# A transformer block on one core: attention jobs of 4 heads x 256 queries, softmax denominators inverted on a reshaped tile by way of DRAM, b2 on GpSimd, last chunk split in two

## The chip, the cores and the metric

The kernel runs on one core of a Trainium2 chip. Times are device microseconds (us) of one execution. "Before" has a median of 1203.07 us over three runs (1201.48 to 1203.55). Engines: PE is TensorE (PEld its weight loads), DVE is VectorE, ACT is ScalarE, POOL is GpSimd, SP is SyncE, which here issues every DMA.

## The reference

One pre-norm transformer block in bf16 with S = 2048 tokens, D = 1024, 32 heads of 32, F = 3584:

```python
h  = x + softmax(q @ k.T * 32**-0.5) @ v @ wo        # q, k, v from layernorm(x) @ wqkv, per head
h2 = h + gelu_tanh(layernorm(h) @ w1 + b1) @ w2 + b2
```

## The kernel before

The kernel is a list of tasks with dependencies. A small scheduler inside the kernel plays them through with assumed durations, and from that fixes the order in which each engine executes its tasks. On the chip every engine then works off its own list in that order, waiting on semaphores.

Attention runs in chunks of 512 queries. Under the attention of one chunk, PE also does "background" work: the projections (chunk 0), then Wo, layer norm, FFN1 and FFN2 of the chunk before. The background has one PSUM bank (7). The last chunk's Wo and FFN run alone after attention: the tail. One attention job is 2 heads x 512 queries. A PV unit is four concurrent matmuls of 512 columns: two for O, two (with a stationary tile of ones) for the softmax denominators.

```python
    def proj(which, g, tc, bank, evac, direct=False):
        ...                                     # psum -> stg (bf16), then for K:
            for pr in range(2):
                for half in range(2):           # four 64x256 copies into KT2
                    dve(lambda v, pr=pr, half=half: v.tensor_copy(
                        KT2[64 * half:64 * half + 64, 2 * g + pr, tc, :, :],
                        stg[64 * pr:64 * pr + 64, s, 256 * half:256 * half + 256]), ...)
        ...
        def pv_unit(self, bank, first, last):
            ...
            for j in range(2):
                fns.append(lambda p, j=j, h=h: p.matmul(psum[32 * j:32 * j + 32, bank, :],
                    V[:, kt, 32 * h:32 * h + 32], PT[:, s, j, :], ...))
            for j in range(2):
                fns.append(lambda p, j=j: p.matmul(psum[64 + 32 * j:96 + 32 * j, bank, :],
                    ones32[:, :], PT[:, s, j, :], ...))
            ...
        def finish(self, qc, g, pr, bank):
            dve(... Dsb[64 * pr:64 * pr + 64, :] <- psum[64:128, bank, :] ...)     # shortened
            dve(... Osb[64 * pr:64 * pr + 64, :] <- psum[0:64, bank, :] ...)       # shortened
            if (qc, g, 1 - pr) in self.fin:
                for k in range(4):
                    dve(lambda v, k=k: v.reciprocal(Dsb[:, 128 * k:128 * k + 128], Dsb[:, 128 * k:128 * k + 128]), 0.93, ...)
                ...
                    dve(lambda v: v.tensor_tensor(OT[:, qc % 2, g, :], Osb[:, :], Dsb[:, :], ALU.mult), ...)
    ...
    def ffn2(R, qc, banks):
        ...                                     # b2 enters as one more matmul of each group
                mm(bank, two_row[:, :], b2t[:, 512 * j:512 * j + 512], True, False, ...)
```

The softmax here doesn't subtract the row's maximum and nothing guards it: scores larger than these inputs give would overflow.

## Time and profile before

The profile of before: per-core view (span, granted clock):

```profile
core 0: 1417.9 us, clock 0.749
```

and the first part of its page (busy us, share of the span, instructions):

```profile
PE 1366.2 (96%) x17326; PEld 510.9 (36%) x17336; DVE 673.2 (47%) x1165; ACT 1085.3 (77%) x1189; POOL 37.9 (3%) x96
```

In that profile PE is the limit, but the span is 215 us longer than the timed runs, so it does not show what limits those. The timeline (start, duration, instruction, count, idle time before) shows Exps back to back at 16.60 / 18 = 0.922 us.

```profile
1238.44 16.60 ACT L643 ACTIVATE PT<-ps 128x1024 bf16<-128x1024 f32 x18 [0.22 <-PE ps L634]
```

The chain of waits (start, duration, what) shows 13 groups of four concurrent 256-column matmuls in 1.92 us (0.148 each), and 49 full 512-column matmuls in 14.08 us (0.287 each):

```profile
93.05 1.92 PE ps L439 x52
...
1328.24 14.08 PE ps L443 x49
```

```profile
PE 1126.7 (94%) x17326; PEld 465.2 (39%) x17336; DVE 668.4 (56%) x1165; ACT 1059.2 (88%) x1189; POOL 38.2 (3%) x96
```

The last PV matmul of this profile ends at 1074.0 us. The windows view splits the span there: attention, then the tail (each entry is the engine's busy time in the window):

```profile
core 0: us, PE busy (x) PEld busy (x) DVE busy (x) ACT busy (x) POOL busy (x), PEclk, DMA share, GB/s
25.00:1074.00 1049.00, 991.55 (x16506) 396.06 (x16495) 578.60 (x989) 1013.24 (x1120) 23.41 (x56) 1.00 0.31 92
1074.00:1201.00 127.00, 114.46 (x533) 52.89 (x539) 71.08 (x130) 37.89 (x60) 6.45 (x16) 0.96 0.28 87
```

Under attention ACT is busy 1013 of 1049 us and PE 992: both are nearly full, and neither has room for much more. In the tail PE alone carries the time.

### The profile page before, as it was taken

How to read it: one execution, taken by the hardware profiler on the slowest of the kernel's cores; microseconds unless marked ns; L12 is line 12 of the kernel's file. 1: busy time of each engine (PE TensorE's matmuls, PEld its weight loads, DVE VectorE, ACT ScalarE, POOL GpSimd, SP SyncE). 2: the span in 40 equal slices, each digit the busy share in tenths (PEclk: the TensorE clock that was granted, in tenths of full speed). 3: DMA queues.
4: the chain of work that ended last, by engine and by line, in shares of the span. 5: the costliest groups of instructions: out<-in, count | busy, mean ns of one | idle time of the engine just before them, and what ended most of it. 6: DMA issues, size and time to landing. Idle time of an engine off the chain costs nothing.

```text
span 1417.9 us, 37847 instructions
## 1 busy us (share of the span) xinstructions
PE 1366.2 (96%) x17326; PEld 510.9 (36%) x17336; DVE 673.2 (47%) x1165; ACT 1085.3 (77%) x1189; POOL 37.9 (3%) x96
## 2 busy tenths in 40 slices
PE   8999999999999999999999999999999999978999
PEld 5544443433333333332333333333333333324333
DVE  7354444443546774223547762225677612245710
ACT  4778787878888888888888888888988888844500
POOL 2000000000100000000100000000000000001000
PEclk7777777777777777777777777777777777766777
DMA  6800000025343222303342230422323322202222
GB/s 165 224 2 13 28 13 14 13 72 156 101 122 101 76 69 72 124 16 98 107 124 71 83 98 16 124 71 63 107 73 98 102 66 85 87 0 75 74 93 71
DMA packets 165793, 112.29 MB, mean 79 GB/s; under 512 B 25345, under 2 KB 162817, under 8 KB 164866
## 3 DMA queue, kind: packets, MB, share of 16 engines
q1 hardware_dynamic: 165634, 109.87, 26.2%
q8 instruction: 136, 2.23, 0.7%
q14 instruction: 23, 0.19, 0.1%
HBM read 98.58 MB, written 11.27 MB: 77 GB/s over the span
## 4 chain that ended last, share of the span: by engine, by line
PE 91%; ACT 4%; DVE 3%; issue 1%; POOL 1%; DMA 0%; POOLq 0%; DVEq 0%
PE ps L439 48%; PE ps L654 17%; PE ps L634 12%; PE ps L443 10%; ACT PT L643 3%; PE ps L658 2%; PE ps L798 1%; ACT xnT L512 1%; DVE a_xh L748 1%; PE ps L508 1%; DVE V L606 0%; DVE stg L547 0%; DVE Osb L668 0%; DVE Dsb L666 0%; DMA a_w1r<-in_A_wqkv_dram 0%
## 5 line engine op out<-in xcount | busy, mean ns | idle before, releaser
L643 ACT ACTIVATE PT<-ps 128x1024 bf16<-128x1024 f32 x1024 | 989.2, 1025 | 180.5 <-PE ps L634 166.1
L654 PE MATMUL ps<-PT,V 128*32 128x512 bf16 x2048 | 383.4, 457 | 13.7 <-DVE V L606 6.2
L658 PE MATMUL ps<-PT,ones 128*32 128x512 bf16 x2048 | 384.8, 458 | 0.0
L439 PE MATMUL ps<-a_w2r,gT 128*32 128x512 bf16 x2688 | 241.9, 452 | 0.0
L634 PE MATMUL ps<-QT,KT 32*128 32x512 bf16 x2048 | 216.7, 414 | 7.4 <-ACT PT L643 7.3
L439 PE MATMUL ps<-a_hnT,a_w1r 128*32 128x512 bf16 x2688 | 215.2, 454 | 4.0 <-DVE a_xh L748 3.2
L654 PEld LDWEIGHTS ps<-PT,V 128*32 128x32 bf16 x2048 | 103.3, 104 | 143.9 <-issue 89.3
L634 PEld LDWEIGHTS ps<-QT,KT 32*128 32x128 bf16 x2048 | 51.5, 91 | 272.3 <-ACT PT L643 164.5
L439 PE MATMUL ps<-xnT,Wall 128*32 128x512 bf16 x1344 | 111.6, 453 | 7.0 <-ACT xnT L512 4.8
L439 PEld LDWEIGHTS ps<-a_w2r,gT 128*32 128x32 bf16 x2688 | 77.3, 109 | 112.0 <-issue 103.3
L673 DVE RECIPROCAL Dsb<-Dsb 128x128 f32<-128x128 f32 x128 | 115.1, 928 | 1.0
L439 PEld LDWEIGHTS ps<-a_hnT,a_w1r 128*32 128x32 bf16 x2688 | 70.6, 107 | 108.0 <-issue 71.4
L782 DVE SCALAR_TENSOR_TENSOR a_ost<-ps,hch 128x512 bf16<-128x512 f32 x24 | 16.6, 692 | 189.8 <-PE ps L439 189.7
L658 PEld LDWEIGHTS ps<-PT,ones 128*32 128x32 bf16 x2048 | 103.5, 104 | 6.6 <-issue 6.6
L748 DVE TENSOR_SCALAR a_xh<-ps,b1f 128x512 bf16<-128x512 f32 x84 | 63.1, 751 | 81.3 <-PE ps L439 80.2
L666 DVE COPY Dsb<-ps 64x512 f32<-64x512 f32 x64 | 44.4, 694 | 101.5 <-PE ps L658 100.1
L439 PE MATMUL ps<-Wall,xnT 128*32 128x256 bf16 x2048 | 83.8, 314 | 0.0
L547 DVE CAST stg<-ps 128x512 bf16<-128x512 f32 x40 | 27.5, 689 | 89.2 <-PE ps L439 89.2
L443 PE MATMUL ps<-a_hnT,b_w1r 128*128 128x512 bf16 x219 | 64.5, 470 | 2.1 <-ACT a_hnT L512 1.5
L439 PEld LDWEIGHTS ps<-Wall,xnT 128*32 128x32 bf16 x2048 | 57.6, 107 | 22.7 <-issue 11.3
L443 PE MATMUL ps<-a_w2r,gT 128*128 128x512 bf16 x219 | 64.1, 461 | 0.5
L439 PE MATMUL ps<-a_w1r,OT 128*32 128x512 bf16 x768 | 63.1, 453 | 0.8 <-DVE hch L719 0.5
(69 smaller groups left out, 875.5 us busy)
## 6 DMA issues: line engine op xcount, KB each, us to landing
a_w2r<-in_B_w_dram SPq DMA_DIRECT2D x56, 512.0 KB, 4.6
a_w1r<-in_B_w_dram SPq DMA_DIRECT2D x42, 512.0 KB, 3.9
a_w1r<-in_A_wo_dram SPq DMA_DIRECT2D x16, 512.0 KB, 4.7
QT<-q_scratch SPq DMA_DIRECT2D x60, 128.0 KB, 2.8
b_w1r<-in_B_w_dram SPq DMA_DIRECT2D x14, 512.0 KB, 3.8
a_w1r<-in_A_wqkv_dram SPq DMA_DIRECT2D x11, 512.0 KB, 5.1
xrb<-in_A_x_dram SPq DMA_DIRECT2D x16, 256.0 KB, 3.9
Wall<-in_A_wqkv_dram SPq DMA_DIRECT2D x16, 256.0 KB, 5.4
```

What stands on the lines that cost most here:

```text
L439: fns.append(lambda p, j=j: p.matmul(psum[32 * j:32 * j + 32, bank, c0:c1], lhsT[:, 32 * j:32 * j + 32], rhs, start=start, stop=stop, tile ...
L443: pe(lambda p: p.matmul(psum[:, bank, c0:c1], lhsT, rhs, start=start, stop=stop), occ, reads=reads, writes=[B_ps[bank]], mode="full")
L508: pe(lambda p, dc=dc: p.transpose(psb[:, bank, dc * P:(dc + 1) * P], src_ap[:, dc * P:(dc + 1) * P], ident[:]), 0.064, reads=[B_src, B_ide ...
L547: dve(lambda v: v.tensor_copy(stg[:, s, :], psum[:, bank, :]), c_dve_ps(512), reads=[B_ps[bank]], writes=[B_stg[s]])
L634: return p.matmul(psum[:, 2 * u + j, :], KT2[r0:r0 + 32, p16, tc, i, :], QT2[r0:r0 + 32, qs, pr, :], start=True, stop=True, tile_position= ...
L643: act(lambda a, u=u, s=s: a.activation(PT[:, s, :, :], psum[:, 2 * u:2 * u + 2, :], ACT.Exp, bias=0.0, scale=SCALE), 1024, reads=[B_ps[2 * ...
L654: fns.append(lambda p, j=j, h=h: p.matmul(psum[32 * j:32 * j + 32, bank, :], V[:, kt, 32 * h:32 * h + 32], PT[:, s, j, :], start=first, st ...
L658: fns.append(lambda p, j=j: p.matmul(psum[64 + 32 * j:96 + 32 * j, bank, :], ones32[:, :], PT[:, s, j, :], start=first, stop=last, tile_po ...
L666: dve(lambda v: v.tensor_copy(Dsb[64 * pr:64 * pr + 64, :], psum[64:128, bank, :]), c_dve_ps(512), reads=[B_ps[bank]], writes=B_Dsb[pr], p ...
L673: dve(lambda v, k=k: v.reciprocal(Dsb[:, 128 * k:128 * k + 128], Dsb[:, 128 * k:128 * k + 128]), 0.93, reads=[B_Dsb[0][k], B_Dsb[1][k]], w ...
L748: dve(lambda v, i=i, fc=fc, bank=bank: v.tensor_scalar(R.xh[:, i, :], psum[:, bank, :], b1f[:, fc:fc + 1], None, ALU.add), c_dve_ps(512), ...
L782: dve(lambda v, o=o, t4=t4, j=j, bank=bank: v.scalar_tensor_tensor(R.ost[:, o, :], psum[:, bank, :], 0.5, hch[:, t4, 512 * j:512 * j + 512 ...
```

## The change

The intent, item by item:

- **Shape.** A job is 4 heads x 256 queries. K and Q are used as projected (no K/Q copies on DVE). O fills columns 0 to 255 of a bank and the denominators columns 256 to 511, on the same partitions, so one DVE copy evacuates both. Matmuls have 256 columns, and there are twice as many.
- **Reciprocals.** A DVE reciprocal of 128x128 takes 0.928 us in before, one of 128x8 takes 0.200 us in after. The 4 x 256 distinct denominators of a job are therefore written to DRAM, read back as 128 x 8, inverted, written again, and read back broadcast.
- **b2** is added by GpSimd instead of by a matmul.
- **Split.** The last chunk of 512 becomes two of 256, to halve the tail.

```diff
+    CH = [(0, 512), (512, 512), (1024, 512), (1536, 256), (1792, 256)]
     ... (proj, load_q, qk, wo, ln2, ffn1 follow the new shapes; cut)
         def pv_tile(self):
+            for den in range(2):
+                for h in range(4):
+                    fns.append(lambda p, h=h, den=den: p.matmul(
+                        psum[32 * h:32 * h + 32, job.bank, 256 * den:256 * den + 256],
+                        ones32[:, :] if den else V[:, kt, P * job.g + 32 * h:P * job.g + 32 * h + 32],
+                        PT[:, ss[h // 2], h % 2, 256 * i:256 * i + 256], ...))
         def finish(self, job):
+            dve(lambda v: v.tensor_copy(OD[:, o, :], psum[:, job.bank, :]), ...)
+            if qc == LAST and g == G - 1:
+                ...                     # the very last jobs still invert on DVE: 2 x 128x128
+                return
+            dma(dd[n].rearrange("(h t) -> h t", h=4), OD[0:P:32, o, 256:512], 4096, ...)
+            dma(Rc[:, o, :], dd[n].rearrange("(p e) -> p e", p=P), 4096, ...)
+            dve(lambda v: v.reciprocal(Rc[:, o, :], Rc[:, o, :]), 0.15, ...)
+            dma(rd_[n].rearrange("(p e) -> p e", p=P), Rc[:, o, :], 4096, ...)
+            for h in range(4):
+                dma(Rb[32 * h:32 * h + 32, b, :], rd_[n:n + 1, 256 * h:256 * h + 256].broadcast_to((32, 256)), 32768, ...)
+            dve(lambda v: v.tensor_tensor(OT[:, qc % 2, g, c0:c0 + 256], OD[:, o, 0:256], Rb[:, b, :], ALU.mult), ...)
     def ffn2(R, qc, banks):
-                mm(bank, two_row[:, :], b2t[:, 512 * j:512 * j + 512], True, False, ...)
+                dve(... R.th[:, f, :] <- psum * 0.5 + hch ...)          # shortened
+                pool(lambda g, ...: g.tensor_tensor(R.ost[:, o, :], R.th[:, f, :], b2t[:, 512 * j:512 * j + 512], ALU.add), 1.1, ...)
```

## The prediction

> **What bounds it now.** The profiled span is 1417.9 us, the timed median 1203.07. The per-core view gives a granted TensorE clock of 0.749; in the profile PE is the limit: 96% busy, 91% of the chain of waits, ACT 77%. A 512-column matmul takes 0.287 us back to back (49 in 14.08 us). The Trainium skill ("TensorE: Matmul & The Clock Gate", Part 1) gives 2.4 GHz as the full clock and says one or two busy cores never trip its 13/16 limiter; this one-core trace is at 0.75 all the same. I infer that the timed runs have a clock near 1. Estimate then: back-to-back Exp of 128x1024 take 0.922 us (18 in 16.60, timeline), x1024 = 944 us; tanh and evacuations before the tail add about 65; first Exp at 27 us: attention ends no earlier than 1030. The tail (1257 to 1418 in the trace, mostly matmuls) would be 128. That is 1160 of 1203; the other 45 are rounds where PE comes late (QK, two PV groups and about five background groups fill a round as well as two Exps do). So ACT and PE jointly until attention ends, then PE and DVE.
>
> **What the change does.**
> - Exps and matmul columns of attention: unchanged. Twice the matmuls, of 256 columns. Those already ran at 0.148 us per group of four (52 in 1.92 us) against 0.142 ideal: about 12 us more over the PV groups; QK with twice the weight loads 0 to 25 us. Partly behind ACT.
> - DVE: minus 115 us reciprocals, 28 K copies, 44 (one OD copy for Dsb and Osb), plus some 15: 673 to about 500. But waits released by DVE cost PE only 27 us of idle time. Worth 0 to 12 us.
> - b2: 32 matmul groups less, 7 to 9 us, a quarter in the tail; the add goes to idle POOL.
> - Reciprocal via DRAM: four dependent transfers of about 2 us (128 KB landed in 1.7 to 2.8 here), 9 us per job of 16. Off the path, except that SyncE is blocked meanwhile.
> - Last chunk split: hoped for, half a tail (60 us). But PE has little room under attention: in the new instruction order, after the last attention matmul there remain 64 group equivalents of narrow FFN1, 112 of narrow FFN2, 32 of Wo and 224 of the last FFN: 432 against 521. Narrow FFN1 has one bank and 2.7 us of DVE per two blocks, so 22 us; then 31 + 3; last FFN1 (14 x 2.25 us, DVE-bound) 32; FFN2 24; end 5: 118 against 128. The layer-norm gap (1270 to 1284) is filled by the FFN2 before it. About 10 us, not 60.
> - Head: first Exp 1 to 2 us earlier.
>
> **Sum.** 1203 - 10 (tail) - 2 - 5 (b2 in attention) - 6 (DVE) + 10 (smaller matmuls) = 1190 us, 8 in 10 between 1160 and 1222. Faster by over 2%: 0.30; within 2%: 0.62; slower: 0.08. In a profile at clock 0.75, about 1410.
>
> **What shows it.** DVE near 500 us; reciprocal group under 20; Exp group near 990; PV within 5% of before; QK under 0.1 us longer per round; after the last Exp still over 130 us at clock 0.75, with narrow FFN matmuls in it; POOL adds near 1 us; OT product about 10 us behind the OD copy.
>
> **What would make it wrong.** Timed clock not near 1; 256-column matmuls bound by weight loads or issue at full clock (slower by 30 us or more); Q loads stuck behind the reciprocal chain on SyncE; or the shorter DVE queue and single evacuation removing most of the 45 us of late rounds (faster, to 1160).

## More of the kernel before

After the prediction I took another profile of the unchanged kernel; it fell at clock 0.993 and is the one to compare with:

```profile
core 0: 1200.7 us, clock 0.993
```

## The result, and the profile after

After has a median of 1223.35 us (1219.28 to 1223.96, four runs); before, beside it, 1202.89. The ratio is 1.016 (95% interval 1.0143 to 1.0178). A ratio here is the mean time of one kernel's fast runs over that of the other's of the same rounds, so it is not quite the ratio of the medians. After is 20 us slower, just above the range I gave, and clear of the noise. All outputs are right.

The profile of after, same three views as for before:

```profile
core 0: 1217.5 us, clock 0.988
```

```profile
PE 1130.9 (93%) x24704; PEld 593.1 (49%) x24704; DVE 524.8 (43%) x976; ACT 1048.7 (86%) x1173; POOL 74.9 (6%) x126
```

```profile
25.00:1094.00 1069.00, 1007.85 (x23056) 515.86 (x23052) 438.39 (x804) 1017.21 (x1124) 54.63 (x88) 0.99 0.34 100
1094.00:1218.00 124.00, 102.19 (x1360) 61.40 (x1348) 66.00 (x126) 22.62 (x39) 12.33 (x16) 0.95 0.61 187
```

The last PV matmul ends at 1094.4 us, 20.4 us later than before; the tail is 123.1 us instead of 126.7. The loss lies under attention. There ACT has 4 us more work and PE 16 us more, but the window is 20 us longer, and DVE, which had been the target of the saving, is busy 140 us less. An engine with less to do cannot be the cost by its own busy time, so one looks for who waits.

The fourth part of the page (shares of the chain that ended last, by engine), before at clock 0.993:

```profile
PE 74%; ACT 11%; DVE 11%; DMA 2%; issue 1%; POOL 1%; SPq 0%; POOLq 0%; DVEq 0%
```

and after:

```profile
PE 61%; DMA 17%; DVE 10%; ACT 6%; SPq 4%; issue 2%; POOL 0%; POOLq 0%; DVEq 0%; ACTq 0%
```

DMA and SyncE's queue went from 2% to 21% of the chain. DVE's waits in after (who waited for what: us in total, times, longest):

```profile
DVE OT L697 <- DMA Rb<-r_scratch: 149.4, 53, 9.2
DVE Rc L692 <- DMA Rc<-d_scratch: 96.7, 43, 8.6
```

DVE stands still for 246 us on the chain through DRAM. DVE's idle time as such costs nothing. What matters is whether something urgent stands behind the waiting instruction. The timeline of after shows that it can:

```profile
501.96 0.39 PE L445 MATMUL ps<-a_w2r,gT 128*32 128x512 bf16 x4
...
502.50 0.40 PE L639 MATMUL ps<-QT,KT 32*128 32x256 bf16 x8
503.55 0.42 DVE L697 TENSOR_TENSOR OT<-OD,Rb 128x256 bf16<-128x256 f32 x1 [9.22 <-DMA Rb<-r_scratch]
503.90 0.68 DVE L806 SCALAR_TENSOR_TENSOR a_th<-ps,hch 128x512 f32<-128x512 f32 x1
504.50 0.68 DVE L679 COPY OD<-ps 128x512 f32<-128x512 f32 x1
504.63 0.83 PE L445 MATMUL ps<-a_w2r,gT 128*32 128x512 bf16 x12 [1.74 <-DVE a_th L806]
```

The background group in bank 7 (L445) is finished at 502.35. Its evacuation (L806) could start then, but on DVE it stands behind the OT product (L697), which has waited 9.22 us for its transfer and starts at 503.55. So the bank comes free over 1 us late, and PE's next background matmul starts at 504.63 after 1.74 us of idle time. The Trainium skill ("TensorE: Matmul & The Clock Gate", section "Architectural detail: the array is 16x 32x32, not 1x 128x128") says that ACT and DVE queues are strict FIFO; this trace agrees, since nothing passed the waiting product. A count over the trace finds about 20 such places under attention, with over 0.3 us between the end of the last background matmul and its evacuation behind an OT product or Rc reciprocal that had waited for its transfer; they add up to about 18 us.

The second pattern is at the start of a chunk, where Wo of the chunk before begins with the last head group (g = 7). The chain of waits in after at 550 us:

```profile
550.12 0.69 DVE a_th L806
550.82 0.61 DVE OD L679
551.42 0.02 issue
551.44 1.85 DMA d_scratch<-OD
553.29 0.02 issue
553.30 2.09 DMA Rc<-d_scratch
555.40 0.02 issue
555.42 0.21 DVE Rc L692
555.63 0.02 issue
555.65 1.63 DMA r_scratch<-Rc
...
558.60 2.69 DMA Rb<-r_scratch
...
561.41 0.43 DVE OT L697
561.84 0.04 issue
561.89 1.46 PE ps L445 x9
```

From the start of the OD copy to the OT product it takes 10.6 us: four dependent transfers of 1.6 to 2.7 us, and 1.3 us in which SyncE issues the first three of the four broadcasts before the last can start. This was one of the shorter chains: the 53 OT products that waited for their transfer started 9.0 to 18.7 us after the end of their OD copy, 12.0 in the median. Until 561.89 PE has no background matmul; it does only QK and PV, has idle gaps, and runs at half clock for 6.8 us from 557.7 us of the span (the records of the granted clock; 10.2 us more from 817.1, at the next chunk start). No single idle gap of PE from 30 us to the end of attention is longer than 2.0 us; in the 3.4 us before each of these two stretches PE was busy for 1.8 us. ACT stays busy until near the end of the first stretch; between 563 and 565 us it does nothing. PE is busy for 1008 of the 1069 us of attention already, so postponed background work comes back later, as Exps that wait for QK or as a longer tail.

### The profile page after: what moved, and what is told of

It reads as the page before. It is cut to its first block, busy times and chain, and to the rows that moved or that the text cites. A ratio compares the mean times of both kernels' runs of the same rounds, so it can differ in the third digit from the quotient of the medians.

```text
span 1217.5 us, 52938 instructions
## 1 busy us (share of the span) xinstructions
PE 1130.9 (93%) x24704; PEld 593.1 (49%) x24704; DVE 524.8 (43%) x976; ACT 1048.7 (86%) x1173; POOL 74.9 (6%) x126
## 4 chain that ended last, share of the span: by engine, by line
PE 61%; DMA 17%; DVE 10%; ACT 6%; SPq 4%; issue 2%; POOL 0%; POOLq 0%; DVEq 0%; ACTq 0%
PE ps L445 37%; PE ps L664 11%; PE ps L639 9%; DMA Rb<-r_scratch 5%; ACT PT L651 4%; DMA r_scratch<-Rc 4%; SPq L466 4%; DMA Rc<-d_scratch 3%; PE ps L449 3%; DVE a_xh L769 3%; DMA d_scratch<-OD 2%; DVE a_uu L778 1%; ACT xnT L516 1%; DMA a_w2r<-in_B_w_dram 1%; PE ps L824 1%
## 5 line engine op out<-in xcount | busy, mean ns | idle before, releaser
L664 PE MATMUL ps<-PT,V 128*32 128x256 bf16 x4096 | 257.3, 275 | 16.1 <-ACT PT L651 11.5
L664 PE MATMUL ps<-PT,ones 128*32 128x256 bf16 x4096 | 256.0, 274 | 0.0
L445 PE MATMUL ps<-a_hnT,a_w1r 128*32 128x512 bf16 (+1 forms) x3584 | 202.3, 354 | 25.8 <-DVE a_xh L769 24.1
L445 PE MATMUL ps<-a_w2r,gT 128*32 128x512 bf16 x3136 | 218.9, 381 | 3.5 <-DVE a_th L806 2.8
L639 PE MATMUL ps<-QT,KT 32*128 32x256 bf16 x4096 | 204.7, 274 | 7.2 <-ACT PT L651 6.5
L445 PEld LDWEIGHTS ps<-a_hnT,a_w1r 128*32 128x32 bf16 x3584 | 84.3, 96 | 105.4 <-DVE a_xh L769 33.0
L445 PEld LDWEIGHTS ps<-a_w2r,gT 128*32 128x32 bf16 x3136 | 71.8, 96 | 66.4 <-issue 29.8
L769 DVE TENSOR_SCALAR a_xh<-ps,b1f 128x512 bf16<-128x512 f32 (+1 forms) x112 | 76.4, 682 | 52.2 <-PE ps L445 51.1
L445 PE MATMUL ps<-xnT,Wall 128*32 128x512 bf16 x1344 | 89.2, 381 | 7.7 <-ACT xnT L516 5.1
L697 DVE TENSOR_TENSOR OT<-OD,Rb 128x256 bf16<-128x256 f32 x63 | 26.8, 425 | 149.5 <-DMA Rb<-r_scratch 149.4
L780 ACT ACTIVATE a_th<-a_uu 128x512 f32<-128x512 bf16 x98 | 62.1, 634 | 33.8 <-DVE a_uu L778 33.5
L809 POOL TENSOR_TENSOR a_ost<-a_th,b2t 128x512 bf16<-128x512 f32 x28 | 32.5, 1161 | 667.1 <-DVE a_th L806 656.9
L445 PE MATMUL ps<-Wall,xnT 128*32 128x256 bf16 x2048 | 70.2, 274 | 2.7 <-DVE V L603 2.3
L782 DVE SCALAR_TENSOR_TENSOR gT<-a_th,a_xh 128x512 bf16<-128x512 f32 x98 | 66.7, 681 | 7.2 <-ACT a_th L780 6.7
L778 DVE SCALAR_TENSOR_TENSOR a_uu<-a_sq,a_xh 128x512 bf16<-128x512 bf16 x98 | 67.6, 690 | 2.6
L445 PE MATMUL ps<-a_w1r,OT 128*32 128x512 bf16 x896 | 62.9, 397 | 5.9 <-DVE OT L697 4.4
L679 DVE COPY OD<-ps 128x512 f32<-128x512 f32 x64 | 43.9, 687 | 39.2 <-PE ps L664 38.3
L445 PEld LDWEIGHTS ps<-Wall,xnT 128*32 128x32 bf16 x2048 | 50.0, 96 | 16.9 <-issue 9.0
```

The lines of the kernel that those rows point to most:

```text
L445: fns.append(lambda p, j=j: p.matmul(psum[32 * j:32 * j + 32, bank, c0:c1], lhsT[:, 32 * j:32 * j + 32], rhs, start=start, stop=stop, tile ...
L639: return p.matmul(psum[:, 2 * us[h // 2] + h % 2, 256 * i:256 * i + 256], KT[32 * h:32 * h + 32, NCH * job.g + tc, P * k4:P * k4 + P], QT[ ...
L664: fns.append(lambda p, h=h, den=den: p.matmul(psum[32 * h:32 * h + 32, job.bank, 256 * den:256 * den + 256], ones32[:, :] if den else V[:, ...
L679: dve(lambda v: v.tensor_copy(OD[:, o, :], psum[:, job.bank, :]), c_dve_ps(512), reads=[B_ps[job.bank]], writes=[B_OD[o]], prio=-1)
L769: dve(lambda v, i=i, fc=fc, bank=bank, c=c: v.tensor_scalar(R.xh[:, i, c], psum[:, bank, c], b1f[:, fc:fc + 1], None, ALU.add), c_dve_ps(w ...
L778: dve(lambda v, i=i: v.scalar_tensor_tensor(R.uu[:, i, :], R.sq[:, i, :], C2, R.xh[:, i, :], ALU.add, ALU.mult), c_dve(512), reads=[R.B_sq ...
```

## The experiments

Time of the n-th Exp's start (us), read from the traces; every kernel has 1024 Exps of the same size, 256 of them per 512 queries. The last columns are the end of the last PV matmul and the tail after it.

| profile of | Exp 1 | 257 | 513 | 769 | 1024 | last PV ends | tail |
|---|---|---|---|---|---|---|---|
| before (clock 0.993) | 23.9 | 299.9 | 557.6 | 815.1 | 1070.6 | 1074.0 | 126.7 |
| after | 22.4 | 297.5 | 560.8 | 829.1 | 1092.7 | 1094.4 | 123.1 |
| e1 reciprocals on DVE | 22.2 | 295.0 | 555.8 | 813.0 | 1072.1 | 1074.4 | 119.6 |
| e4 longer latencies | 21.8 | 294.1 | 552.0 | 810.7 | 1073.6 | 1076.0 | 128.0 |
| e5 product and reciprocal on GpSimd | 22.3 | 295.4 | 558.4 | 820.5 | 1086.2 | 1088.3 | 124.9 |
| e6 e1 without split | 22.1 | 294.6 | 552.5 | 809.3 | 1064.9 | 1066.8 | 125.1 |
| e7 shape alone | 22.0 | 294.4 | 552.5 | 808.8 | 1064.5 | 1066.5 | 125.3 |
| e8 = e4 + g = 7 on DVE | 21.7 | 296.1 | 554.0 | 814.6 | 1077.0 | 1079.2 | 113.5 |
| e10 g = 7 on DVE | 21.9 | 296.5 | 559.5 | 825.0 | 1089.8 | 1091.8 | 112.4 |
| e11 = e5 + e10 | 22.5 | 299.4 | 560.8 | 820.5 | 1085.5 | 1087.5 | 110.4 |

After is not behind until Exp 257, that is while chunk 0 runs with projections in the background; it loses from the first chunk start on.

My theory at this point: the reciprocal's way through DRAM is the loss. Rivals: the split with its extra weight traffic (132 MB moved on the DMA queue against 110), or the 256-column matmuls. One thing holds for every experiment: the scheduler builds the order of all engines anew, so each edit also reshuffles instructions that it does not name. e2 and e3 below, which leave the chain alone, moved the time by 0 and 2.5 us; gains of 10 us and more are well above that, differences of a few us are not.

**b0_before: before unchanged, for a profile at the same clock.**

> The kernel before, unchanged, for a profile at the same granted clock as the one of after (0.99). All theories: about 1202 us, clock over 0.97. My estimate was that its tail (from the last PV matmul to the end) is 128 us, so attention ends near 1075 us; after has 123 and 1094. If attention here ends near 1075, the loss of the change (about 20 us) lies wholly under attention, and the tail gained about 5 us. If it ends near 1095, the loss lies in the tail. [...]

Measured: 1202.52 us (one run, so of unknown state), clock 0.993, attention to 1074.0, tail 126.7. The loss lies under attention. (This run has two half-clock stretches as well, but elsewhere: from about 1067 us, where attention ends, and from about 1090 us, in the tail.)

**e1_recip: reciprocals on DVE.**

```diff
-            dma(dd[n]...); dma(Rc[:, o, :]...); dve(reciprocal Rc); dma(rd_[n]...); 4 x dma(Rb[...])
+            for k in range(2):
+                dve(lambda v, k=k: v.reciprocal(Rb[:, b, P * k:P * k + P], OD[:, o, 256 + P * k:256 + P * k + P]), 0.93, ...)
```

> After, with the reciprocals on DVE again (two of 128x128 per job, 0.93 us each) in place of the four dependent transfers through DRAM. Theory 1 (the reciprocal's way through DRAM delays OT at chunk starts and blocks SyncE's queue): 1190 to 1205 us, 20 to 30 us faster than after, the clock dips at chunk starts gone. Rival 2 (the split last chunk and its weight traffic cost the time): within 8 us of 1223. Rival 3 (256-column matmuls are what costs): within 8 us of 1223, or slower because DVE gets 105 us more work.

Measured: 1193.99 us, ratio to before 0.9931 (0.9914 to 0.9948). Against after that is 0.0229 of 1203, or 27.5 us, with 93 us more work on DVE:

```profile
PE 1125.1 (94%) x24701; PEld 594.9 (50%) x24704; DVE 617.6 (52%) x1039; ACT 1046.3 (88%) x1173; POOL 74.5 (6%) x126
```

The theory's number came in. Not quite as forecast: two dips of the clock remain, from 304.6 and 799.5 us of the span, 3.4 us each. The dips are not the cause of the loss: 17.0 us at half clock under attention (after) cost PE at most 8.5 us of full-clock time, and e11 below has 20.4 us of them and no loss.

**e2_nosplit: four chunks of 512 again.**

```diff
-    CH = [(0, 512), (512, 512), (1024, 512), (1536, 256), (1792, 256)]
+    CH = [(0, 512), (512, 512), (1024, 512), (1536, 512)]
```

> After, with four chunks of 512 again (only the split of the last chunk undone). Rival 2 (the split costs: 20 MB more weights, DMA waits of 5 to 7 us in the tail, single-bank FFN1 after the last attention): 1200 to 1210 us. Theory 1 (DRAM reciprocal): 1222 to 1235 us, because the split as such saved about 5 to 10 us. Rival 3 (256-column shape): the same 1222 to 1235.

Measured: 1220.97 us, ratio 1.0161, the same as after's 1.0160. The rival that blames the split falls (1220.97 is also 1 us under the band of the theory). So does my own estimate that the split saves 5 to 10 us; e6 takes that up.

**e3_b2mm: b2 as a matmul again.**

```diff
+                mm(bank, two_row[:, :], b2t[:, 512 * j:512 * j + 512], True, False, ...)
-                pool(... R.ost <- R.th + b2t ...)
```

> After, with b2 as a matmul again (32 more groups of 512 columns, no GpSimd add). All theories: 1223 to 1232 us, 0 to 9 us slower than after (40 groups of 0.22 us are 8.8 us if all on the path). If it is faster, the GpSimd add (1.16 us, behind a DVE instruction in the ring of th) was itself a cost.

Measured: 1219.91 us, ratio 1.0139 (1.0119 to 1.0158). The interval overlaps that of after, and 1219.91 is just under the forecast band, so b2's move is worth nothing that these runs resolve, and certainly not the 7 to 9 us I had estimated. (The 40 groups in the expectation are a slip for 32.)

**e4_lat: the same instructions, in an order built on longer latencies.** Only the scheduler's assumption is changed, by 1.5 us for each of the chain's transfers:

```diff
-            t.done = max(state["dma"], s0) + dma_lat - 0.9
+            t.done = max(state["dma"], s0) + dma_lat - 0.9 + t.extra      # extra = 1.5 for the chain's DMAs
```

> After with no instruction changed: only the scheduler is told that each of the chain's transfers takes 1.5 us longer than it assumed, so that the small reciprocal and the OT product stand later in DVE's fixed order, and the dependent transfers later in SyncE's. e1 (reciprocals on DVE) showed that the way through DRAM costs 29 us. Theory 1a (the loss is head-of-line blocking: DVE idles 246 us behind late transfers, with evacuations of the background bank behind it, because the order was built on too short a latency): 1198 to 1212 us, DVE's wait for Rb and Rc falls below 100 us. Theory 1b (the loss is the latency of the chain itself, OT late at chunk starts and at the end): 1218 to 1235 us, as now or worse.

Measured: 1204.35 us, ratio 1.0008 (0.9993 to 1.0023): 18.3 us faster than after with the same instructions in another order. DVE's waits on the chain halved:

```profile
DVE OT L700 <- DMA Rb<-r_scratch: 70.6, 25, 5.9
...
DVE Rc L695 <- DMA Rc<-d_scratch: 45.8, 17, 7.5
```

They sum to 116 us, a little over the 100 that I had written. Two thirds of the loss went away with an order that was built for a longer chain. The order of after was built for about 9 us from OD copy to last landing (the scheduler's 2.1 us for each transfer, plus its size), against the median of 12.0 measured in after. e4's 6 us more lie above that median, so the "true latencies" of the expectation for e8 are latencies with a margin; how large a margin is best was not tried. The table shows where the remaining 10 us are: attention ends nearly as in e1, but the tail is 8 us longer. In the order as built, 82 group equivalents (of 512 columns) of narrow FFN1 are left for the time after attention, against 58 in e1, because Wo waits for the chain at each chunk start.

**e5_pool: small reciprocal and OT product on GpSimd.** GpSimd is nearly idle, so now waits for the chain hold up DVE only once (an OD copy, 10.3 us, for a buffer that an OT product on GpSimd still reads). The dependent transfers stay on SyncE, with the latencies that the scheduler had assumed. The order is built anew, on SyncE too, and the chain gets longer: from the end of the OD copy to a product that waited, 13.6 us in the median against 12.0 in after.

```diff
-            dve(lambda v: v.reciprocal(Rc[:, o, :], Rc[:, o, :]), 0.15, ...)
+            pool(lambda g: g.tensor_tensor(Rc[:, o, :], Rc[:, o, :], cexp[:, 8:16], ALU.pow), 1.65, ...)
-            dve(lambda v: v.tensor_tensor(OT[...], OD[:, o, 0:256], Rb[:, b, :], ALU.mult), c_dve(256), ...)
+            pool(lambda p, g=g: p.tensor_tensor(OT[...], OD[:, o, 0:256], Rb[:, b, :], ALU.mult), 0.6, ...)
```

> After with the small reciprocal (as a power of -1) and the OT product on GpSimd, which is idle, so that waits for the DRAM chain block no DVE instruction; SyncE's queue and the length of the chain stay (the chain becomes 2 us longer). Theory 1a, DVE's part (DVE stalls behind late transfers): 1195 to 1210 us. Rival (SyncE blocked, or the chain's length): 1218 to 1235 us. Between 1210 and 1218: both.

Measured: 1213.5 us, ratio 1.0078 (1.0057 to 1.0099), 9.9 us faster than after and in the band that I had called "both". The waits moved to an engine on which they block little:

```profile
POOL Rc L692 <- DMA Rc<-d_scratch: 387.3, 61, 37.8
POOL OT L697 <- DMA Rb<-r_scratch: 361.8, 61, 11.1
```

GpSimd now waits 749 us, three times what DVE did in after, and the kernel is faster.

**e6_recip_nosplit: e1 with four chunks of 512.** The edits of e1 and e2 together.

> e1 (reciprocals on DVE, 1194 us) with four chunks of 512 again. It prices the split without the chain's disturbance. My estimate of the split was 10 us: 1199 to 1206 us. If the split is worth nothing, as undoing it in after suggested (1221 against 1223): 1192 to 1197.

Measured: 1194.39 us, ratio 0.9926, equal to e1's 0.9931. The two profiles show how the split comes to nothing. e1, attention and tail:

```profile
25.00:1074.00 1049.00, 1004.64 (x23124) 519.46 (x23116) 534.33 (x875) 1015.38 (x1125) 54.35 (x88) 1.00 0.31 94
1074.00:1194.00 120.00, 99.65 (x1284) 59.32 (x1276) 63.22 (x120) 21.91 (x38) 12.30 (x16) 0.95 0.62 189
```

and e6:

```profile
25.00:1067.00 1042.00, 993.32 (x22536) 505.98 (x22528) 509.87 (x828) 1011.68 (x1119) 51.52 (x80) 0.99 0.30 90
1067.00:1192.00 125.00, 112.60 (x522) 51.36 (x529) 68.86 (x125) 38.00 (x60) 15.37 (x24) 0.96 0.29 89
```

The split takes PE work out of the tail (113 to 100 us busy) and puts it under attention (993 to 1005 us), where PE and ACT are both nearly full, so attention becomes 7.6 us longer and the tail 5.5 us shorter.

**e7_shape_only: e6 with b2 as a matmul.** What is left of the change is the shape of the attention jobs. The edits are those of e1, e2 and e3 together.

> Reciprocals on DVE, four chunks of 512, b2 as a matmul: what is left of the change is the shape of the attention jobs (4 heads x 256 queries, O and denominators in one bank, no K/Q copies). If 256-column matmuls cost PE nothing that shows and the freed DVE work shows little: 1198 to 1208 us, within 6 us of before (1202) and 0 to 8 us above e6. If the shape is a loss: over 1210.

Measured: 1193.98 us, ratio 0.9924 (0.9909 to 0.9939). This is below the forecast band of 1198 to 1208. The shape alone is worth 0.0076 of 1203, or 9 us; b2's place is again worth nothing (e7 and e6 differ by 0.0002). More than half of the gain is there by the end of the projection stage. Before at clock 0.993, 25 to 300 us:

```profile
25.00:300.00 275.00, 256.39 (x5000) 122.46 (x4992) 141.04 (x300) 251.20 (x269) 4.93 (x8) 1.00 0.25 73
```

and e7:

```profile
25.00:300.00 275.00, 262.15 (x6644) 153.20 (x6640) 106.57 (x165) 255.47 (x273) 4.94 (x8) 1.00 0.24 72
```

With the K/Q copies and the second evacuation gone, DVE has 34 us less to do there, PE and ACT are fuller by 4 to 6 us, and the kernel is 5.5 us ahead at Exp 257 (299.9 against 294.4; 1.9 of it at the first Exp already); afterwards the lead stays at 5 to 6 us.

**e8_lat_g7: e4, with the g = 7 jobs of every chunk inverted on DVE.**

```diff
-            if qc == LAST and g == G - 1:
+            if g == G - 1:                  # on top of e4
```

> e4 (the scheduler told the true latencies, 1204 us) with the last head group of every chunk (g = 7, the one whose OT the next Wo waits for first) done by the DVE reciprocal; the other seven keep the way through DRAM. It tests what the 10 us between e4 and e1 (1194) are. Theory (the chain's length at chunk starts keeps Wo back and pushes background work behind the end of attention; e4 ends with 82 group equivalents of narrow FFN1 there, e1 with 58, this one with 46): 1188 to 1197 us. Rival (the chain's transfers disturb all jobs, not just the last of a chunk): 1200 to 1206.

Measured: 1193.7 us, ratio 0.9925 (0.9907 to 0.9943). So the 10 us between e4 and e1 come from the g = 7 jobs, whose OT the next Wo needs first, and not from the chain in the other jobs. They are gained in the tail: e8 has 14.5 us less of it than e4, and 3.2 us more of attention.

**e9_lat_g7_nosplit: e8 with four chunks of 512.**

> e8 with four chunks of 512. If the split only moves time from the tail into attention (e1 against e6: 5.5 us less tail, 7.6 us more attention), the same as e8 within 3 us: 1187 to 1197. It is also the candidate for the best version: at least as fast as e7 (1194) if DVE's 90 us less work is worth anything.

Measured: 1199.16 us, ratio 0.9974 (0.9959 to 0.9989), out of the expected band: here the split is worth 6 us. Its tail is 125.9 us and e8's 113.5; its attention ends at 1073.5 and e8's at 1079.2. So the split trades 12.4 us of tail against 5.7 of attention here, and 5.5 against 7.6 between e1 and e6. What the trade yields depends on how much background work still fits under attention (e8 leaves 46 group equivalents of FFN1 after it, e1 leaves 58). "The split is worth nothing" therefore holds for after and e1, not in general.

**e10_g7: after with only the g = 7 jobs on DVE**, the latencies as they were (the edit line of e8, on after).

> After with only the g = 7 jobs done by the DVE reciprocal, the scheduler's latencies as they were. If the two parts add (order built on too short a latency 19 us, chain length at chunk starts 10 us): 1209 to 1215 us. If the chunk starts were the whole loss: 1192 to 1200. If they are no part of it: 1219 to 1225.

Measured: 1207.0 us, ratio 1.0047 (1.0028 to 1.0066): 13.6 us faster than after, slightly below the band for two parts that add. The traces show the wait that is gone: at the chunk starts near 550 and 810 us, from the end of the last OD copy to the first Wo matmul, after takes 10.5 and 11.4 us and e10 2.0 and 2.0. Most of the gain then appears in the tail:

```profile
25.00:1092.00 1067.00, 1012.74 (x23300) 523.22 (x23296) 458.46 (x835) 1018.33 (x1128) 54.46 (x88) 1.00 0.34 101
1092.00:1204.00 112.00, 93.78 (x1085) 54.36 (x1088) 56.62 (x108) 20.18 (x35) 12.32 (x16) 0.96 0.62 189
```

Attention ends 2.6 us earlier than in after, and the tail is 10.7 us shorter, because less narrow FFN1 is left for it: counted in the traces, 32 group equivalents in e10 and 64 in after.

**e11_pool_g7: e5 and e10 together.** But for one OD copy (6.6 us) no DVE instruction waits for the chain, and no chunk start waits for it. The assumed latencies stay; the expectation says that SyncE's order stays too, but it was built anew.

> After with both: the small reciprocal and the OT product on GpSimd (e5, 1213.5: no DVE instruction waits for the chain), and the g = 7 jobs by the DVE reciprocal (e10, 1207). SyncE's order, built on the short latencies, stays. If DVE's stalls and the chunk starts are the whole loss: 1190 to 1199. If SyncE's blocked queue costs something of its own: 1201 to 1207, and the rest up to e8 (1194) is SyncE's.

Measured: 1194.94 us, ratio 0.992 (0.9901 to 0.9939): 28.9 us faster than after, which is the whole loss. SyncE is blocked as long as in after: its waits for the chain's steps (OD copy, first transfer, Rc, third transfer) sum to 434 us here and to 435 us in after. The two largest in after:

```profile
SPq L466 <- DVE OD L679: 193.2, 46, 17.2
SPq L466 <- DVE Rc L692: 90.7, 50, 5.2
```

and in e11:

```profile
SPq L466 <- DVE OD L679: 149.4, 36, 18.1
SPq L466 <- POOL Rc L692: 134.4, 42, 7.4
```

So the blocked queue costs nothing in total that these runs resolve. The way to the total is another than in e1, though: attention ends 13 us later (1087.5 against 1074.4) and the tail is 9 us shorter (110.4 against 119.6), with 32 group equivalents of narrow FFN1 left for it against 54. What holds attention back in e11 was not looked into.

Everything beside each other, with the gain over after as the difference of the two ratios times 1203 us:

| kernel | median us | ratio to before | gain over after, us |
|---|---|---|---|
| after | 1223.35 | 1.0160 | |
| e2 no split | 1220.97 | 1.0161 | -0.1 |
| e3 b2 as matmul | 1219.91 | 1.0139 | 2.5 |
| e5 product and reciprocal on GpSimd | 1213.50 | 1.0078 | 9.9 |
| e10 g = 7 on DVE | 1207.00 | 1.0047 | 13.6 |
| e4 longer latencies in the scheduler | 1204.35 | 1.0008 | 18.3 |
| e9 e8 without split | 1199.16 | 0.9974 | 22.4 |
| e11 = e5 + e10 | 1194.94 | 0.9920 | 28.9 |
| e6 e1 without split | 1194.39 | 0.9926 | 28.2 |
| e7 shape alone | 1193.98 | 0.9924 | 28.4 |
| e1 reciprocals on DVE | 1193.99 | 0.9931 | 27.5 |
| e8 = e4 + g = 7 on DVE | 1193.70 | 0.9925 | 28.3 |

e1, e6, e7, e8 and e11 beat both kernels, by 0.7 to 0.8% over before, and are not told apart. The simplest is e7: the new shape and nothing else. Two of them (e8, e11) keep most of the DRAM chain and spare DVE 87 us or more of busy time against e1 (e8: 531 us, e1: 618); it buys nothing.

## Why the prediction was wrong, point by point

- **What failed: the step "Reciprocal via DRAM: four dependent transfers of about 2 us (...), 9 us per job of 16. Off the path, except that SyncE is blocked meanwhile."** The length was near for a quiet chain (10.6 us from the OD copy to the OT product at 550 us, with transfers of 1.6 to 2.7 us) and a third too short for the median one (12.0). The conclusion "off the path" was wrong by 28 us (e1). I compared the chain with the job period and asked whether it keeps up, instead of asking who stands behind it. There are two such places. DVE's fixed order puts the small reciprocal and the OT product where the scheduler expected their data, and the evacuation of the one background bank stands behind them: 10 us when that is removed (e5). And Wo of each chunk waits for the last job's chain: 14 us when that is removed (e10). Removed together they give 29 us. That is 5 more than the sum of each alone, but the four intervals put about 4.6 us of noise on that difference, and e5 made the chain longer where Wo waits for it, so an interaction of the two is not shown.
- **SyncE's blocked queue,** which I named as the exception and again among what could go wrong ("Q loads stuck behind the reciprocal chain on SyncE"), was the wrong engine: e11 leaves SyncE waiting for the chain as long as in after (434 and 435 us) and has no loss left.
- **The inference of the clock near 1 held.** The profile of after has 0.988, and before at 0.993 has attention to 1074 and a tail of 127 us; I had estimated the tail at 128 and the time in attention by difference. "ACT and PE jointly until attention ends" is what the windows show.
- **Tail: "118 against 128. About 10 us, not 60."** The tails are 123.1 and 126.7; against e1, where the chain does not disturb, 119.6. That the split would not halve the tail was right, and for the reason given. But the term was mis-sized, because I let the work that leaves the tail vanish: it lengthens attention by 7.6 us (e1 against e6), so the sum is zero there, and in e8 against e9 it is 6.
- **b2: "32 matmul groups less, 7 to 9 us":** 0 to within these runs (e6 against e7, and e3). The groups are gone, but I have not shown where their 7 us went. That 24 of the 32 lie under attention, where ACT is as full as PE, and that a GpSimd add of 1.16 us now follows the last evacuation, are arguments only.
- **"About 12 us more over the PV groups; QK (...) 0 to 25 us":** no cost shows. From start to start the traces give 0.33 us for a QK round and 0.23 us for a single PV unit of 512 columns, with 512-column matmuls (before at clock 0.993) and with 256-column ones (after) alike. (The "0.142 ideal" is an estimate: 256 columns at 0.749 of the 2.4 GHz that the prediction cites.)
- **DVE "minus (...): 673 to about 500 (...). Worth 0 to 12 us":** DVE did fall to 525 us. The reciprocals' share of that was worth nothing that shows (e8 and e11 save most of it against e1 and take the same time). The copies' share and the earlier first Exp (1.5 to 1.9 us, as predicted) are the likely parts of the 9 us of the shape (e7): 5.5 us are there by Exp 257. How the 9 us divide is not shown.
- **The sum.** Without the DRAM chain the change takes 1194 us (e1), beside the predicted 1190. That is luck in part: tail, b2 and smaller matmuls were each off by 5 to 10 us and cancelled. The missing term of 28 us is what put the result outside.
- **What stays open:** how e4's 18 us divide between DVE and PE. Its longer assumed latency moves waiting DVE instructions back, but also lets PE do other background work at the chunk starts. And I have not tried the chain's DMAs on another queue.

## What to carry to other kernels

Before an instruction is made cheaper by a round trip through memory, ask what stands behind it on every engine that waits for the trip: on an in-order engine a 10 us wait costs whatever urgent work queues there, even if the engine is half idle. Where a kernel's order comes from a cost model, give the model latencies measured under load; here 1.5 us more per transfer in the model was worth 18 us on the chip with the same instructions. And work moved from a tail under a stage where two engines are already full is paid there; price both sides.

## What the Trainium skill lacked or had wrong

- "TensorE: Matmul & The Clock Gate", Part 1, gives 13/16 as the limited clock, with one or two busy cores never tripping it, and otherwise 4/8 and 8/8. The first profile here, one core, was granted 0.752 for 1242 us on end and the same kernel later 1.0. No page has that state, so a profile's clock has to be read before its shares are believed. The half-clock stretches of after (6.8 and 10.2 us) are multiples of the page's 3.4 us window; there the trace agrees.
- "DMA: Bandwidth & Descriptors", "Anatomy of one DMA", gives about 2.0 us fixed per DMA for the GpSimd path. The small transfers here, issued from SyncE, took 1.85, 2.09, 1.63 and 2.69 us one after the other at 551 to 561 us, which agrees. Under the load of the rest of the kernel the second step took more: from issuing the 4 KB read to the small reciprocal that waited for it, 1.5 to 6.1 us in after, 2.1 in the median. SyncE's issuing stood on the chain as well: four broadcasts took 1.72 us, 0.43 each.
- No page warns that a schedule fixed ahead on that 2 us is fragile on strict-FIFO engines. Number: DVE waited 246 us in after, and 18 us of the time came back by assuming 1.5 us more per transfer (e4).
- "TensorE: Matmul & The Clock Gate", Part 3, gives speedups of row and column tiling for 512 columns. It has none for 256. No run here has an unpacked matmul to compare with, so a speedup is not shown; the time of a packed group is the same in both forms, 0.33 us for a QK round and 0.23 us for a PV unit of 512 columns.
